# Attention feeding a gated FFN on one core: the last q slice in a lent PSUM bank, and k^T v joined to q times k^T v

## The chip, the cores and the metric

The kernel runs on one core of one Trainium2 chip. The core has five engines with queues of their own: TensorE (PE; PEld is its weight load), VectorE (DVE), ScalarE (ACT), GpSimd (POOL) and SyncE (SP), which only issues DMAs. On-chip memory is SBUF, 128 partitions; matmul results go to PSUM, whose banks hold 128 x 512 float32 each. The metric is the device time of one execution in microseconds, the lower the better.

## The reference

Eight batches of eight heads, 576 positions, head width 64. There is no softmax: k^T v is formed first, q is multiplied with it, each 64-wide row is normalised, and the result, heads side by side, is the input of a gated FFN (512 wide, 1536 inside, 4608 tokens in all).

```python
kv = np.einsum('bhsd,bhse->bhde', k, v)
out = np.einsum('bhsd,bhde->bhse', q, kv)
rms = np.sqrt(np.mean(out * out, axis=-1, keepdims=True) + 1e-06)
out = out / rms * g_norm
# (B,H,S,D) -> (B*S, H*D)
gate = 1.0 / (1.0 + np.exp(-(x @ w_gate)))
val = x @ w_val
return (gate * val @ w_out)
```

q, k and v come as 32-bit floats; the weights come as 64-bit floats, which the kernel converts itself.

## The kernel before

**The FFN.** The tokens are cut into nine chunks of 512 (`c` = 0 to 8). Chunk 0 goes through plain products (128x512 instructions, L599 and L833) while VectorE and ScalarE convert the weights, a step at a time (`CV`, the lines L197 to L237). Chunks 1 to 8 use a bilinear scheme with fewer multiplications: `first_layer_fast` runs three blocks `j` of 26 products each (list `PRODUCTS1`, four 128x256 instructions a product, L957), numbered p = 26 j + i from 0 to 77; `second_layer_fast` runs 26 longer products (L1059). Each product accumulates into a region, a PSUM bank named by a letter A to K; a region's bank is taken from the left of a deque `free` of five banks at its first product, and given back at the right after its last use. After each product, `combine` writes the steps listed with it: copies out of PSUM on ScalarE (L923; `o3=B` is one), sigmoids on ScalarE (L916), sums on VectorE (L927), multiplications on GpSimd (L919). GpSimd also forms the sums of h that the second layer multiplies (`h_sums`, L733), and in chunk 1 some of the sums of the output weights (`w_form`: L1030 on either engine, L1032 on VectorE alone).

**Attention.** Batch 0 is done at the start, head pair by head pair. Batches 1 to 7 are done inside the FFN of an earlier chunk: batches 1 and 2 begin in chunk 0, batch c + 1 runs in chunk c. `feed(b)` makes the steps. A batch is worked in two runs `m` = 0, 1 of four heads each:

- `load_q_run` loads q of one run into a tile: 32-column pieces of two head pairs, so that one 32x32-block transpose on VectorE turns them; behind these 2 S columns lie 2 HD more, a second copy of the last two rows of each group, of the head pair that otherwise lies on the upper 64 partitions (L119, L120). `load_late` loads k and v of the next batch into h_more, which later holds sums of h.
- `kv_mm` forms k^T v of all eight heads in one tile `at` of three PSUM banks: 64 instructions of 128x64 (the mains, L389), then 16 of 64x64 (the rest of the rows, L396). `kv_copy` brings it to SBUF on ScalarE, once whole (L404) and once more from the upper 64 partitions to the lower (L405). `kv_set_aside` (batch 2) copies it to a place of its own first (L400).
- `turn` transposes q (L408; the second copy L410).
- `u_mm` multiplies (L439): nine slices of 128 rows for each of two head pairs `g` and each half `e`, 64x64 matmuls. Head pair g sits on partitions 64 g to 64 g + 63, hence on that row half of the array; e sets the column half. Slices 0 to 7 of g = 0 land in one bank, those of g = 1 in the next; the last slices of both land side by side in the third, and the last slice of g = 1 is taken from the second copies of q and k^T v, on row half 0.
- `u_square` squares the whole of u (L444, ScalarE, PSUM to SBUF), `u_sum` sums over 64 (L447), `u_root` takes the root, and the normalisation and the transposes to the FFN's layout follow.

**What sets the order.** No scheduler moves anything; the code runs in the order in which the program writes it, engine by engine. Around the change three lists set it: `places` (chunk 0: "44:KV2,ASIDE" is the step list behind the 44th plain product instruction), `where` (from batch 2 on: "28:u0" puts u of run 0 behind product 28 of the first layer), and the list `forms` of chunk 1 (product, sum, engine). Each step that an engine is not ready for makes it wait, and what stands behind waits too.

Of the kernel before, what the change touches and what calls it, by code (L numbers as in the profile page):

```python
# [10 lines left out]
FP32 = mybir.dt.float32  # L11
# [9 lines left out]
def kernel(  # L21
# [32 lines left out]
    JR = S // QB  # L54
    NSL = JR // 2
    NRUN = NHP // 2
    QW = 2 * S + 2 * HD

    NK4 = S // P
    S4 = P * NK4  # L60
# [44 lines left out]
    def load_q_run(b, m):  # L105
        if b >= B:
            return
        if b == 1:
            t = h_main[2 - m].rearrange("p s c -> p (s c)")[:, 4 * NT * P - QW:4 * NT * P]
        else:  # L110
            t = sb.tile([P, QW], FP32, tag="q", name="q", bufs=1)
        main = t[:, 0:2 * S].rearrange("p (e j c) -> p e j c", e=2, c=QB)
        more = t[:, 2 * S:QW].rearrange("p (e j c) -> p e j c", e=2, c=QB)
# [152 lines left out]
    g_col = const.tile([P, 1], FP32, name="g_col")  # L266


    kvq = const.tile([P, 2, NRUN, 2, HD], FP32, name="kvq")
# [20 lines left out]
    def attention(n, at_ps):  # L290

        b, m = divmod(n, NHP)
        d = {}
        kv = kvq[:, 0, m // 2, m % 2]

        def kv_mm():
            d["kv"] = ps = at_ps("kv")
# [78 lines left out]
    def feed(b):  # L376

        d = {}

        def kv_mm():  # L380

            mains, rest = kv_late[b]
            d["kv"] = ps = at_ps()[:, 0:NRUN, 0:2 * HD].rearrange("p m (e d) -> p m e d", d=HD)
            for m in range(NRUN):
                for e in range(2):
                    for j in range(NK4):
                        for g in range(2):
                            c = slice(NK4 * HD * e + HD * j, NK4 * HD * e + HD * j + HD)
                            nc.tensor.matmul(ps[HD * g:HD * g + HD, m, e], mains[2 * m + g, "k"][:, c],  # L389
                                             mains[2 * m + g, "v"][:, c],  # L390
                                             start=(e == 0 and j == 0), stop=False, skip_group_check=True)
            for e in range(2):
                for m in range(NRUN):
                    for g in range(2):
                        rs, c = slice(PH * m, PH * m + PH), HD * (2 * g + e)
                        nc.tensor.matmul(ps[HD * g:HD * g + HD, m, e], rest[rs, c:c + HD],  # L396
                                         rest[rs, GH + c:GH + c + HD], start=False, stop=True, skip_group_check=True)

        def kv_set_aside():
            nc.scalar.copy(out=kv_ahead, in_=d["kv"])  # L400
            d["kv"] = kv_ahead

        def kv_copy():
            nc.scalar.copy(out=kvq[:, 0], in_=d["kv"])  # L404
            nc.scalar.copy(out=kvq[0:HD, 1], in_=d["kv"][HD:P])  # L405

        def turn(m, e):
            nc.vector.transpose(qTs[:, S * e:S * e + S], q_late[b, m][:, S * e:S * e + S])  # L408
            if e == 1:
                nc.vector.transpose(qTs[0:HD, 2 * S:QW], q_late[b, m][0:HD, 2 * S:QW])  # L410
                if b > 1:
                    load_q_run(b + (m + 1) // NRUN, (m + 1) % NRUN)
                elif m == NRUN - 1:
                    load_q_run(b + 1, 0)

        def heads_run(m):
# [6 lines left out]
            def place(g, s_):  # L423
                return (NSL - 1) * g + s_ if s_ < NSL - 1 else 2 * (NSL - 1) + g
# [2 lines left out]
            def by_head(t):  # L427
                return t.rearrange("p (n d) -> p n d", d=HD)

            def u_mm():  # L430
                d["u"] = u = at_ps().rearrange("p r c -> p (r c)")[:, 0:2 * S]
                for t in range(NSL + 1):
                    for g in range(2):
                        if t < NSL - 1 or g == 0:
                            head, s_ = (1, NSL - 1) if t == NSL else (g, t)
                            o = HD * place(head, s_)
                            for e in range(2):
                                c = 2 * S + HD * e if t == NSL else S * e + HD * s_
                                nc.tensor.matmul(u[HD * e:HD * e + HD, o:o + HD],  # L439
                                                 qTs[HD * g:HD * g + HD, c:c + HD],  # L440
                                                 kvq[HD * g:HD * g + HD, t == NSL, m, e], start=True, stop=True)

            def u_square():
                nc.scalar.activation(out=sq, in_=d["u"], func=AF.Square)  # L444

            def u_sum(i):
# [44 lines left out]
        kv = [kv_mm, kv_copy, kv_set_aside] if b == 2 else [kv_mm, kv_copy]  # L491
        t0, t1 = ([lambda m=m, e=e: turn(m, e) for e in range(2)] for m in range(NRUN))
        u0, u1 = heads_run(0), heads_run(1)
        if b == 1:
            return kv, t0 + t1 + u0 + u1, ()
        n_ = "n{0}0 n{0}1 n{0}2 n{0}3 n{0}4 n{0}5 n{0}6" if b == 2 else "n{0}0 n{0}1"
# [71 lines left out]
    def at_ps():  # L568
        return psum.tile([P, NAT, 512], FP32, tag="at", name="at")
# [212 lines left out]
    def w1_form(c, j, part, v):  # L782
        if c == 1:
# [13 lines left out]
    named = {"LL": lambda: load_late(1), "LL2": lambda: load_late(2), "KV": batch1[0][0], "KV2": second_batch[0][0],  # L797
             "W0": lambda: w1_sums(0), "W1": lambda: w1_sums(1),
             "ASIDE": second_batch[0][2], "CV": convert_step}
    named.update({"C": batch1[0][1], "D": second_batch[0][1]})  # L800
    for i in range(NRUN):
        named[f"Q{i}"] = lambda i=i: load_q_run(1, i)
        named.update({f"t{i}{e}": batch1[1][2 * i + e] for e in range(2)})
    for i, which in enumerate("ab"):
        for n, step in enumerate(("u", "sq", "s0", "s1", "rt", "rc", "n0", "n1", "n2", "x0", "x1")):
# [326 lines left out]
    for c in range(1, NG):  # L1132
        at1, at2 = {}, {}
        for p, step in x_late:
            at1.setdefault(p, []).append(step)
        x_late = []
        if c + 1 < B:
            kv, first_, then = second_batch if c == 1 else feed(c + 1)
            for p, step in (list(zip((21, 22) if c == 2 else (19, 20), kv)) if c > 1 else []) + first_:
                at1.setdefault(p, []).append(step)  # L1140
            for p, step in zip((3, 6) if c == 1 else (4, 6), then):
                at2.setdefault(p, []).append(step)
        if c + 1 < NG:
            for n, p in enumerate(X1 if c == 1 else X2 if c + 1 < B else X3):
                step = lambda n=n, c=c: x_sum(c + 1, n)
                if p < NPR:
                    at2.setdefault(p, []).append(step)
                else:
                    x_late.append((p - NPR, step))
        if c == 1:  # L1150
            for at_, forms in ((at1, ((28, 9, 0), (30, 10, 0), (34, 12, 0), (52, 11, 1), (53, 22, 0), (57, 14, 0), (58, 8, 1), (61, 19, 0), (64, 16, 1))), (at2, ((1, 13, 0), (3, 23, 0), (4, 25, 1), (9, 15, 0), (10, 24, 0), (10, 20, 0), (11, 17, 0), (12, 18, 0), (13, 21, 0)))):
# [36 lines left out]
```

## Time and profile before

| | |
|---|---|
| time, median of 3 runs | 1002.54 us (1002.2 to 1002.74) |
| the profiled execution's own time | 1003.68 us |
| its span | 1001.9 us, TensorE's granted clock 1.00 |
| PE busy | 993.2 us, 99% |
| VectorE, GpSimd, ScalarE busy | 723.3, 617.8, 342.2 us |
| chunk 0 from the first q times k^T v, 62.6 to 162 | 99.4 us |
| chunk 1, 162 to 262.57 | 100.57 us |
| chunks 2 and 3 | 106.63 and 106.64 us |

A line of a group reads: line of the kernel, engine, operation, tiles out <- in, shape, count, busy time, mean duration, idle time of the engine ahead of it and what ended it. A line of a tile's answer has the shortest, median and longest duration in ns instead. A line of the waits reads: who waited, for whom, the total in us, how often, and the longest one. A piece of the chain is: start, length, engine and line. A line of a timeline has start and length of a run of instructions of one line, and in square brackets how long its engine idled before it. Several matmuls overlap in the array, so counts and starts tell more of their pace than durations.

### The profile page before, as it was taken

What the parts mean: (1) busy time and instruction counts of PE and PEld (TensorE: products, weight loads), DVE (VectorE), ACT (ScalarE), POOL (GpSimd) and SP (SyncE); (2) the same over time, 40 slices, a digit from 0 to 9 for tenths busy, and PEclk for the clock granted to TensorE, in tenths of its full rate; (3) what the DMA queues carried; (4) which work ended last, traced back from release to release, by engine and by line L of the source; (5) the groups of instructions that cost most, each with busy time, mean ns of one, the idle gap of its engine ahead of it and who ended that gap; (6) DMA issues with size and microseconds to landing.
All of it is one profiled execution on the core that took longest, in us unless ns stands there. A gap on an engine that the chain in (4) does not pass through costs nothing.

```text
span 1001.9 us, 16623 instructions
## 1 busy us (share of the span) xinstructions
PE 993.2 (99%) x5958; PEld 815.9 (81%) x5958; DVE 723.3 (72%) x1199; ACT 342.2 (34%) x606; POOL 617.8 (62%) x991
## 2 busy tenths in 40 slices
PE   8999999999999999999999999999999999999998
PEld 7445447888888888888888888888888888888887
DVE  4889999889757756784677576866587566755672
ACT  4566322652144213530344124421442133213320
POOL 1509997798259633965196708861596349744963
PEclk9999999999999999999999999999999999999999
DMA  9996514764899568746975677756754555444614
GB/s 256 285 263 192 173 42 119 220 220 134 271 294 267 176 183 239 240 158 197 278 220 170 186 218 244 196 171 193 235 198 159 161 176 208 157 148 162 216 50 124
DMA packets 155155, 195.43 MB, mean 195 GB/s; under 512 B 83809, under 2 KB 127841, under 8 KB 155073
## 3 DMA queue, kind: packets, MB, share of 16 engines
q0 software_dynamic: 22128, 114.37, 34.4%
q1 hardware_dynamic: 126864, 78.16, 27.9%
q10 hardware_dynamic: 6080, 1.84, 0.8%
q8 instruction: 47, 0.77, 0.3%
q14 instruction: 36, 0.29, 0.1%
HBM read 160.50 MB, written 25.56 MB: 186 GB/s over the span
## 4 chain that ended last, share of the span: by engine, by line
PE 94%; POOL 2%; DMA 1%; ACT 1%; SPq 1%; issue 1%; DVE 1%; POOLq 0%; ACTq 0%; DVEq 0%
PE mm L957 51%; PE mm L1059 27%; PE mm L599 8%; PE mm L833 4%; PE at L439 2%; PE at L389 1%; DMA v<-in_v_dram 1%; PE at L599 1%; POOL h_more L733 1%; POOL h L733 1%; POOL h L919 0%; POOL w L1030 0%; SPq L93 0%; PE at L396 0%; DVE sg L927 0%
## 5 line engine op out<-in xcount | busy, mean ns | idle before, releaser
L957 PE MATMUL mm<-xs,w 128*128 128x256 f32 x1428 | 331.9, 380 | 0.0
L957 PEld LDWEIGHTS mm<-xs,w 128*128 128x128 f32 x1428 | 270.4, 190 | 37.4 <-DVE sg L927 0.4
L957 PE MATMUL mm<-xT,w 128*128 128x256 f32 x948 | 229.8, 380 | 0.0
L957 PEld LDWEIGHTS mm<-xT,w 128*128 128x128 f32 x948 | 179.5, 190 | 25.0 <-issue 0.2
L780 POOL DMA_DIRECT2D w<-kept x84 | 46.7, 556 | 192.5 <-PE mm L957 188.5
L927 DVE TENSOR_TENSOR sg<-sg,mm 128x512 f32<-128x512 f32 (+1 forms) x176 | 100.8, 600 | 85.0 <-PE mm L957 40.3
L1059 PE MATMUL mm<-w,h 128*128 128x256 f32 x630 | 142.8, 379 | 0.0
L1059 PEld LDWEIGHTS mm<-w,h 128*128 128x128 f32 x630 | 119.7, 190 | 16.3
L919 POOL TENSOR_TENSOR h<-h,sg 128x512 f32<-128x512 f32 x72 | 96.7, 1360 | 56.4 <-DVE h L927 30.4
L923 ACT COPY temps<-mm 128x512 f32<-128x512 f32 (+1 forms) x128 | 66.1, 538 | 186.7 <-PE mm L1059 94.7
L733 POOL TENSOR_TENSOR h<-h 128x128 f32<-128x128 f32 x216 | 113.1, 535 | 16.5 <-DVE h_more L733 13.1
L1059 PE MATMUL mm<-w,h_more 128*128 128x256 f32 x474 | 108.2, 379 | 0.0
L916 ACT ACTIVATE sg<-sg 128x512 f32<-128x512 f32 x96 | 59.7, 630 | 133.6 <-DVE sg L927 133.6
L1059 PEld LDWEIGHTS mm<-w,h_more 128*128 128x128 f32 x474 | 90.1, 190 | 12.2
L923 ACT COPY sg<-mm 128x512 f32<-128x512 f32 (+1 forms) x112 | 56.9, 510 | 86.4 <-PE mm L1059 45.0
L733 POOL TENSOR_TENSOR h_more<-h 128x128 f32<-128x128 f32 x120 | 61.6, 517 | 35.0 <-DVE h L919 30.8
L927 DVE TENSOR_TENSOR temps<-temps,mm 128x512 f32<-128x512 f32 (+1 forms) x96 | 59.4, 619 | 25.7 <-PE mm L1059 16.5
L599 PE MATMUL mm<-xT,w 128*128 128x512 f32 x176 | 77.8, 596 | 0.1
L927 DVE TENSOR_TENSOR temps<-mm,temps 128x512 f32<-128x512 f32 (+1 forms) x64 | 39.8, 622 | 50.7 <-PE mm L1059 24.3
L923 ACT COPY h<-mm 128x512 f32<-128x512 f32 x48 | 28.1, 585 | 138.3 <-PE mm L957 138.3
L927 DVE TENSOR_TENSOR sg<-mm,sg 128x512 f32<-128x512 f32 (+1 forms) x64 | 39.7, 620 | 46.7 <-PE mm L957 24.7
L599 PEld LDWEIGHTS mm<-xT,w 128*128 128x128 f32 x176 | 32.6, 190 | 39.2 <-issue 36.1
(148 smaller groups left out, 1283.6 us busy)
## 6 DMA issues: line engine op xcount, KB each, us to landing
w<-kept POOLq DMA_DIRECT2D x42, 896.0 KB, 5.4
w<-kept POOLq DMA_DIRECT2D x90, 384.0 KB, 4.8
w<-kept POOLq DMA_DIRECT2D x42, 768.0 KB, 5.0
out_dram<-sg SPq DMA_DIRECT2D x119, 64.0 KB, 1.7
h_more<-in_k_dram SPq DMA_DIRECT2D x28, 256.0 KB, 5.5
h_more<-in_v_dram SPq DMA_DIRECT2D x28, 256.0 KB, 6.2
q<-in_q_dram SPq DMA_DIRECT2D x96, 72.0 KB, 5.0
xT<-xTs SPq DMA_DIRECT2D x96, 72.0 KB, 4.6
```

What stands on the lines that cost most here:

```text
L389: nc.tensor.matmul(ps[HD * g:HD * g + HD, m, e], mains[2 * m + g, "k"][:, c], mains[2 * m + g, "v"][:, c], start=(e == 0 and j == 0), stop ...
L439: nc.tensor.matmul(u[HD * e:HD * e + HD, o:o + HD], qTs[HD * g:HD * g + HD, c:c + HD], kvq[HD * g:HD * g + HD, t == NSL, m, e], start=True ...
L599: nc.tensor.matmul(self.ps[i], w[("wg", "wv")[i], self.f][:, m, :], xT[self.c][:, m, :], start=(m == 0), stop=(m == NMT - 1), skip_group_c ...
L733: ops.append((eng, lambda v=v, x=x, sign=sign, y=y, eng=eng: eng.tensor_tensor(out=h_form(v, j), in0=h_form(x, j), in1=h_form(y, j), op=op ...
L780: nc.gpsimd.dma_start(out=granule(g)[:, 0:n], in_=kept1[g // NPA % N3, g % NPA][:, 0:n])
L833: nc.tensor.matmul(ps[t], gv[0, f][:, P * t:P * t + P], w["wo", f], start=(f == 0), stop=(f == NFT - 1), skip_group_check=True)
L916: nc.scalar.activation(out=o["o" + step[1]], in_=o["o" + step[1]], func=AF.Sigmoid)
L919: mult.tensor_tensor(out=o[x], in0=o[x], in1=o[y], op=ALU.mult)
L923: nc.scalar.copy(out=o[out_], in_=o[expr])
L927: tt(out=o[out_], in0=o[x], in1=o[y], op=ALU.add if sign == "+" else ALU.subtract)
L957: nc.tensor.matmul(regions[name][1][:, g], ws[:, g], xf[c][wv], start=(new and g == 0), stop=True, skip_group_check=True)
L1059: nc.tensor.matmul(regions[name][1], h_form(hv, j), ws[:, j], start=(used[i] and j == 0), stop=(j == N3 - 1), skip_group_check=True)
```

## The change

- q's second copies are no longer loaded or transposed (`QW` = 2 S), nor k^T v's. The last slice of g = 1 goes, like the others of g = 1, through row half 1, into the first 64 columns of another bank: bank 4 for batch 1, and from batch 2 on a bank lent from the deque `free` while u is formed. Just ahead of the square ScalarE copies these 128x64 values to their place beside the others, and the bank goes back to `free`.
- From batch 3 on `kv_mm` and `kv_copy` are no steps of their own; they run inside run 0's `u_mm`, which stands behind product 25 in place of 28 (k^T v stood behind 19, or 21 in chunk 2). The 64x64 part goes first, then the mains of m = 0 and m = 1; m = 0 is formed in the third bank of `at`, m = 1 in the lent bank, beside the slice that will come there. Two 128x128 copies to SBUF follow in place of a 128x256 and a 64x256 copy, and then u. The square stays behind product 30.
- In chunk 0 batch 2's k^T v (KV2) is formed inside `bu` (u of batch 1, run 1), which stands at place 44 in place of 47; the square of it goes to 47, with the setting aside behind it.
- In chunk 1 sum 14 of the output weights (VectorE) stands behind product 55 in place of 57, with its store.

```diff
-    QW = 2 * S + 2 * HD
+    QW = 2 * S
...
-                queue.dma_start(out=more[QB * i:QB * i + QB, e], in_=src[:, JR - 2:JR])
...
-        def kv_mm():
+        def kv_mm(at, lent):
...
+            if at is None:
+                at = at_ps()
+                d["kv"] = ps = [at[:, m, 0:2 * HD].rearrange("p (e d) -> p e d", d=HD) for m in range(NRUN)]
+            else:
+                d["kv"] = ps = [t.rearrange("p (e d) -> p e d", d=HD)
+                                for t in (at[:, NAT - 1, 2 * HD:4 * HD], lent[:, HD:3 * HD])]
...
+            if b > 2:
+                tails(True)
...
         def kv_copy():
-            nc.scalar.copy(out=kvq[:, 0], in_=d["kv"])
-            nc.scalar.copy(out=kvq[0:HD, 1], in_=d["kv"][HD:P])
+            for m in range(NRUN):
+                nc.scalar.copy(out=kvq[:, m], in_=d["kv"][m])
...
-                nc.vector.transpose(qTs[0:HD, 2 * S:QW], q_late[b, m][0:HD, 2 * S:QW])
...
+            def u_mm(first=()):
+                at = at_ps()
+                d["u"] = u = at.rearrange("p r c -> p (r c)")[:, 0:2 * S]
+                i_ = 4 if b == 1 else free.popleft()
+                lent = bank(i_)
+                for step in first:
+                    step(at, lent)
+                for s_ in range(NSL):
                     for g in range(2):
...
+                        o = HD * place(g, s_)
+                        to = lent[:, 0:HD] if s_ == NSL - 1 and g == 1 else u[:, o:o + HD]
...
+                d["lent"] = i_, lent[:, 0:HD], u[:, o:o + HD]
 
             def u_square():
+                i_, lent, to = d["lent"]
+                nc.scalar.copy(out=to, in_=lent)
+                if b > 1:
+                    give(i_)
                 nc.scalar.activation(out=sq, in_=d["u"], func=AF.Square)
...
+            u0[0] = lambda u_mm=u0[0]: u_mm((kv_mm, lambda at, lent: kv_copy()))
+            kv = []
...
-                   5:t00 8:t01 28:u0 29:t10 30:q0 33:s00,s01 36:r0 39:t11 41:n00 47:n01 51:x00,x01 54:u1
+                   5:t00 8:t01 25:u0 29:t10 30:q0 33:s00,s01 36:r0 39:t11 41:n00 47:n01 51:x00,x01 54:u1
...
-                   3:t00 7:t01 28:u0,t10 30:q0,s00,s01 37:r0 39:t11 47:n00,n01 53:x00,x01 54:u1
+                   3:t00 7:t01 25:u0 28:t10 30:q0,s00,s01 37:r0 39:t11 47:n00,n01 53:x00,x01 54:u1
...
-        43:ax1 44:KV2,ASIDE 46:CV,W0 47:bu 48:CV,CV,bsq 50:CV,bs0 52:CV,CV 54:bs1 55:CV,CV,brt,D 57:CV,CV 58:CV 60:CV,brc
+        43:ax1 44:bu 46:CV,W0 47:bsq,ASIDE 48:CV,CV 50:CV,bs0 52:CV,CV 54:bs1 55:CV,CV,brt,D 57:CV,CV 58:CV 60:CV,brc
...
-                    (52, 11, 1), (53, 22, 0), (57, 14, 0), (58, 8, 1), ...
+                    (52, 11, 1), (53, 22, 0), (55, 14, 0), (58, 8, 1), ...
```

More of the change, by code (lines that the diff above doesn't have):

```diff
@@ L266 @@
     g_col = const.tile([P, 1], FP32, name="g_col")
-    kvq = const.tile([P, 2, NRUN, 2, HD], FP32, name="kvq")
+    kvq = const.tile([P, NRUN, 2, HD], FP32, name="kvq")
     kv_ahead = const.tile([P, NRUN, 2, HD], FP32, name="kv_ahead")
@@ L293, in attention @@
         d = {}
-        kv = kvq[:, 0, m // 2, m % 2]
+        kv = kvq[:, m // 2, m % 2]
         def kv_mm():
@@ L378, in feed, with tails @@
         d = {}
-        def kv_mm():
+        def kv_mm(at, lent):
             mains, rest = kv_late[b]
-            d["kv"] = ps = at_ps()[:, 0:NRUN, 0:2 * HD].rearrange("p m (e d) -> p m e d", d=HD)
+            if at is None:
[4 more added lines that the diff above has]
+                                for t in (at[:, NAT - 1, 2 * HD:4 * HD], lent[:, HD:3 * HD])]
+            def tails(first):
+                for e in range(2):
+                    for m in range(NRUN):
+                        for g in range(2):
+                            rs, c = slice(PH * m, PH * m + PH), HD * (2 * g + e)
+                            nc.tensor.matmul(ps[m][HD * g:HD * g + HD, e], rest[rs, c:c + HD],
+                                             rest[rs, GH + c:GH + c + HD], start=first and e == 0, stop=not first,
+                                             skip_group_check=True)
+            if b > 2:
+                tails(True)
             for m in range(NRUN):
@@ L388, in kv_mm @@
                             c = slice(NK4 * HD * e + HD * j, NK4 * HD * e + HD * j + HD)
[L389 to L397, printed above, removed]
+                            nc.tensor.matmul(ps[m][HD * g:HD * g + HD, e], mains[2 * m + g, "k"][:, c],
+                                             mains[2 * m + g, "v"][:, c], start=(b < 3 and e == 0 and j == 0),
+                                             stop=(b > 2 and j == NK4 - 1), skip_group_check=True)
+            if b < 3:
+                tails(False)
         def kv_set_aside():
-            nc.scalar.copy(out=kv_ahead, in_=d["kv"])
-            d["kv"] = kv_ahead
+            for m in range(NRUN):
+                nc.scalar.copy(out=kv_ahead[:, m], in_=d["kv"][m])
+            d["kv"] = [kv_ahead[:, m] for m in range(NRUN)]
         def kv_copy():
-            nc.scalar.copy(out=kvq[:, 0], in_=d["kv"])
-            nc.scalar.copy(out=kvq[0:HD, 1], in_=d["kv"][HD:P])
+            for m in range(NRUN):
+                nc.scalar.copy(out=kvq[:, m], in_=d["kv"][m])
         def turn(m, e):
@@ L804 @@
     for i, which in enumerate("ab"):
-        for n, step in enumerate(("u", "sq", "s0", "s1", "rt", "rc", "n0", "n1", "n2", "x0", "x1")):
+        for n, step in list(enumerate(("u", "sq", "s0", "s1", "rt", "rc", "n0", "n1", "n2", "x0", "x1")))[which == "b":]:
             named[which + step] = batch1[1][2 * NRUN + 11 * i + n]
@@ L1138 @@
             kv, first_, then = second_batch if c == 1 else feed(c + 1)
-            for p, step in (list(zip((21, 22) if c == 2 else (19, 20), kv)) if c > 1 else []) + first_:
+            for p, step in first_:
                 at1.setdefault(p, []).append(step)
```

27 lines of the change are left out of this document (11 added, 16 removed).

## The prediction, made before the result was known

> **What bounds the kernel now.** I read the page's busy shares first, then TensorE's waits, then the chain of waits over one batch, then groups and timelines around the lines that change.
>
> ```profile
> PE 993.2 (99%) x5958; PEld 815.9 (81%) x5958; DVE 723.3 (72%) x1199; ACT 342.2 (34%) x606; POOL 617.8 (62%) x991
> ```
>
> ```profile
> PE mm L652 <- POOL ident masks.py:199: 1.4, 1, 1.4
> PE mm L301 <- DMA v<-in_v_dram: 1.3, 2, 0.8
> ...
> PE mm L957 <- POOL h L733: 0.4, 1, 0.4
> ```
>
> PE is busy 99% of the span, and its waits sum to about 4 us, nearly all before 30 us. After that one wait is left, of 0.4 us, in chunk 1. So from 30 us on only two things count: PE time added or removed, and new PE waits. The chain for chunk 3, start and length in us, is PE alone:
>
> ```profile
> 369.20 17.27 PE mm L957 x80
> 386.47 2.02 PE at L389 x64
> 388.49 0.39 PE at L396 x16
> 388.88 7.97 PE mm L957 x36
> 396.85 1.31 PE at L439 x72
> 398.16 22.64 PE mm L957 x104
> 420.80 1.31 PE at L439 x72
> 422.11 20.05 PE mm L957 x92
> 442.17 33.67 PE mm L1059 x156
> ```
>
> The last line gives 216 ns for one 128x256 instruction (33.67/156). The small matmuls are three trips out of the long stream: one to k^T v (L389, L396), two to q times k^T v (L439). From 369.20 to 442.17 are 72.97 us; 312 product instructions at 0.2158 are 67.33, the small pieces 2.41 + 2 x 1.31 = 5.03; the 0.61 left is the cost of going and returning, **0.20 us a trip**.
>
> ```profile
> L439 PE MATMUL at<-kvq,qTs x1008: 218/218/267, 61.2 to 742.0; 64*64 64x64 f32 x168
> L396 PE MATMUL at<-h_more x112: 218/218/267, 52.9 to 708.6; 64*64 64x64 f32 x112
> L444 ACT ACTIVATE sqs<-at x14: 1130/1131/1137, 62.7 to 742.9; 128x1152 f32<-128x1152 f32 x14
> L404 ACT COPY kvq<-at x6: 350/372/373, 53.7 to 708.8; 128x256 f32<-128x256 f32 x6
> L405 ACT COPY kvq<-at x6: 368/368/369, 54.0 to 709.2; 64x256 f32<-64x256 f32 x6
> ```
>
> One L439 trip is 72 instructions. In the trace's rows the first 64 start in groups of four, a group each 58 ns (16 groups); the last 8 start in pairs, a pair each 58 ns (4 pairs). The pairs are the last slices of the two head pairs, which both go through the array's first 64 rows now.
>
> **The change part by part.** The sum is made against the profiled execution (1003.68 us, span 1001.9, 1.8 around it); the median, 1002.54, is 1.14 below it.
>
> *Last slice through the lent bank.* The last 8 instructions become 2 groups of four, at 2 x 58 = 0.117 us less per trip; 14 trips (2 for each of 7 batches): **-1.64 us**. Bounds: 0 if the two halves don't run side by side into two banks; -1.64 if they do, as the first 16 groups do.
>
> *k^T v joined to u0, batches 3 to 7.* One trip of three goes: -0.20 each, **-1.0 us** for five. The pieces keep their lengths: 64x64 ahead of 128x64, then 64x64 again, has one change of shape more than 128x64 ahead of 64x64. A change costs 0.09 us in the rows (151 ns where 58 is the pitch), and the product after a trip starts 0.10 late; so four changes in place of five and one late product in place of two are again 0.19. In chunk 0 KV2 is joined into bu with its mains still ahead of its tails, so three changes are left of five: 2 x 0.09 for the changes, 0.10 for the late product and 0.05 for the late first group behind a change: **-0.33**.
>
> *What the joined u waits for.* u's first matmul waits for the first k^T v copy on ScalarE. That copy can start when the first run's mains are done, half way through L389's 2.02 us; behind it lie the other 1.0 us of mains, the copy takes under 0.37 (L404 has 256 columns, this 128), and ScalarE's sigmoid before it (393.29 to 393.92) ends with product 25. Cover 1.0 us, need about 0.4: 0. The second copy (128x128, nearest rows L404 372 and L479 342) starts as u starts and is needed only by the last slice, 0.93 us on: 0. Without that cover (u behind both copies) it would be about 0.55 us a batch. GpSimd's first write over k and v in h_more comes 5.9 us after product 25, the reads end at 3: 0.
>
> *Removed.* L405's copies, 7 x 0.37 us of ScalarE, replaced by the second 128x128 copy; 14 transposes at L410 (0.26 us) of VectorE; 56 DMA issues (four for each of 14 runs; 48 on SP's queue with the x stores and out stores behind them, 8 on GpSimd's for batch 1). ScalarE, VectorE and SP are not the bound: 0 here, but VectorE sits 0.26 us earlier behind each.
>
> *Added: 14 copies 128x64 on ScalarE, just ahead of the square.* Duration: 512 columns took 585 ns, 256 took 372, so 64 about 212 (estimate); the nearest row of this size, L479, took 292 to 461. They matter where ScalarE is late. With u at product 25 and the square still at 30, ScalarE runs: copy A, copy C, lent copy, square, copy B (o3=B); and product 32 writes bank B again. In the timeline of chunk 3 before:
>
> ```profile
> 396.88 0.58 ACT L923 COPY h<-mm 128x512 f32<-128x512 f32 x1 [1.14 <-PE mm L957]
> ...
> 398.20 1.13 ACT L444 ACTIVATE sqs<-at 128x1152 f32<-128x1152 f32 x1 [0.74 <-PE at L439]
> ...
> 399.23 0.58 ACT L923 COPY sg<-mm 128x512 f32<-128x512 f32 x1
> ```
>
> The first of these is copy C, the last copy B. Before, u's trip stood between C and product 29 and gave ScalarE 1.5 us. After, on the same clock: C 396.88, lent copy 0.48 later (the pitch of copies), square 0.21 later, B 1.03 later, done 0.58 later: 399.2. Product 32 follows C's product by three products and would have its weights by 399.1: a stall of 0.09 us (0 to 0.25, with the 461 row) each, five times, and once in chunk 1: **+0.54**.
>
> *Chunk 0.* PE saves 2 x 0.117 + 0.33 = 0.57, but the second half of chunk 0 is paced by VectorE's weight conversion (96.37 of 99.40 us busy from 62.6 to 162). The saving lasts only as far as conversion leaves room, about 0.2 us at product 4 of the second layer; and the ASIDE copies and the square now stand ahead of ScalarE's part of one conversion. I keep 0.2 (bounds -0.57 to +0.3 against before): **+0.37** back.
>
> *w_out sum 14, two products sooner in chunk 1.* VectorE, before:
>
> ```profile
> 210.09 1.41 DVE L447 TENSOR_REDUCE ms<-sqs 128x9 f32<-128x576 f32 x2 [1.28 <-ACT sqs L444]
> 211.42 1.95 DVE L1032 SCALAR_TENSOR_TENSOR w<-w,w 128x768 f32<-128x768 f32 x1
> ```
>
> PE's only late wait (a gap of 0.79 where 0.22 is the pitch, so 0.57) is at 226.94 behind a GpSimd sum of h, and that chain starts from VectorE, which runs about 2.6 us late there. After, sum 14 stands ahead of the reduces, in the 1.28 us that VectorE waited. Its other rows took 0.95 and 1.20. If it runs in the gap, VectorE is up to 1.86 us earlier behind it; if it is held until GpSimd's multiplication ends at 209.95, it ends at 210.9 and VectorE is 1.0 earlier. By the first the wait goes wholly; by the second the wait goes too, but narrowly, since PE itself comes 0.34 earlier. The next limit on GpSimd's own chain lies 0.72 below the present one. I take -0.6 for chunks 0 and 1 together, of which 0.2 and 2 x 0.117 - 0.09 are counted above: **-0.26** more.
>
> The Trainium skill, "SBUF — State Buffer", section "Who interferes with whom", has a VectorE instruction with two SBUF inputs blocked by a GpSimd instruction that reads SBUF. This trace bears it out (GpSimd's L1030 sums, 1.8 us elsewhere, took 2.26 beside such work). By it VectorE is 1.0 us earlier, without it 1.86.
>
> **Sum.** -1.64 - 1.0 - 0.33 + 0.54 + 0.37 - 0.26 = -2.3. 1003.68 - 2.3 = 1001.4 by the profile, **1000.2** by the median.
>
> **Rivals.**
> 1. *The wait at 226.94 stays* (another GpSimd sum is late). Then chunks 0 and 1 end where they did, and only the five batches count: 5 x (0.234 + 0.20 - 0.09) = 1.7: **1000.8**. For it: GpSimd works without a break from 216 to 228. Against: its chain hangs on VectorE.
> 2. *Everything pays*: no stall at product 32, and chunks 0 and 1 give all that GpSimd's next limit allows: 5 x 0.434 + 0.72 = 2.9: **999.6**. For it: the stall is 0.1 by the sum, and only if the weights wait and not the product. Against: VectorE in chunk 0 has no room.
> 3. *The halves don't overlap* in the lent bank: -1.64 goes, the lent copy remains: -0.7, **1001.9**. For it: no row shows a group of four into two different tiles. Against: the first groups of four write different banks too.
> 4. *Slower: ScalarE at product 32.* If lent copy and square go one after the other with a wait for PSUM between, or the lent bank comes back late and product 29 has no bank, each batch loses the excess: above 0.46 us per batch (2.3/5) it decides; at 0.8 (one square's remainder and a lost pitch of 0.5) five batches cost 5 x 0.8 - 2.3 = +1.7, and chunk 0's conversion another 0.5: **1004.7**. For it: slack was only 0.1 there. Against: ScalarE is 34% busy, and catches up within two products.
>
> **How the numbers follow.** Forecast 0.45, rival 1 0.20, rival 2 0.10, rival 3 0.08, rival 4 0.17. The forecast's own range is 999.7 to 1000.8 (the stall at 0 to 0.25 six times, rival 1's bound above). The range takes in rivals 1 to 3 and the better part of what lies between 3 and 4, and leaves out most of 4; below, it goes 0.5 past rival 2, for the trip cost being a mean: 999.1 to 1002.9. 0.2% of 1002.54 is 2.0 us, about what can be told from no change: 1000.5 and 1004.5. Faster: two thirds of the forecast, rival 2, and a third of rival 1, 0.47; slower: most of rival 4, 0.13; the rest 0.40.
>
> **What would show it.** L439 1.31 to 1.19 us per trip and 64x64 matmuls in groups of four to the end; one trip fewer in each of chunks 2 to 6, their length 106.63 to about 106.3; ScalarE's B copy ending at product 32's start, with a new PE wait on L923 of about 0.1; no PE wait behind L733 in chunk 1. Wrong if PE's waits list shows L439 behind L404's copies, or any wait over 0.4 us per chunk.

## The result, and the profile after

Measured side by side, 21 executions each, the kernel before took 1003.2 us (median) and the changed one 1000.77 (999.4 to 1003.04); the ratio is 0.9971, 95% interval 0.9964 to 0.9979, which is 2.1 to 3.6 us less on 1002.54. The forecast, 1000.2 from 1002.54, is a ratio of 0.9977. The changed kernel is faster, and inside the range. The measured ratio puts it at 999.6 on the forecast's scale, 2.9 us less; the forecast's 2.3 lies inside the interval too.

The profiled execution of the changed kernel took 1003.04 us, span 1001.3: the slowest of its 21, and only 0.64 us below the one shown of before. So spans of two profiles can't be compared here; the stretches within them can. The line numbers move by the lines that were added: L439 is now L453, L389 L403, L396 L392, L957 L980, L1059 L1082, L923 L946, L927 L950, L733 L755, L444 L462, L1032 L1055; the lent copy is L459. Some of the runs below shift them by a few lines more.

PE is busy 99% of the span, as before. Its waits, after:

```profile
PE two L353 <- DVE sqs L345: 1.5, 1, 1.5
PE mm L674 <- POOL ident masks.py:199: 1.4, 1, 1.4
PE mm L856 <- DVE w L235: 0.6, 2, 0.3
PE two L309 <- DMA q<-in_q_dram: 0.6, 1, 0.6
PE two L326 <- ACT qTs L314: 0.6, 2, 0.3
```

The wait behind GpSimd's h (L733 before) is gone from the list. L856, the plain second layer of chunk 0, waits twice for converted weights, at 117 and 124 us; that is new. The other four stand in the first 25 us, where the kernel before waited in much the same places. The chain over chunk 3, from the first product to the second layer:

```profile
369.76 22.45 PE mm L980 x104
392.21 0.20 PE at L392 x2
...
392.60 1.08 PE at L403 x32
393.68 0.93 PE mm L403 x32
394.62 1.14 PE at L453 x66
...
395.82 25.34 PE mm L980 x116
421.16 1.14 PE at L453 x66
...
422.37 20.05 PE mm L980 x92
```

Two trips where there were three. k^T v (L392, then L403, first into `at`, then into the lent bank, here named mm) runs straight into u (L453), and the last slice alternates between `at` and mm in pieces of two.

Between landmarks in the trace's rows (first product of one layer to the first of the next; chunk 0 from its first k^T v instruction at about 50 us) the two profiled executions compare like this, in us:

| stretch | before | after | difference |
|---|---|---|---|
| chunk 0, from the first k^T v | 106.842 | 108.147 | +1.305 |
| chunk 1, first layer | 71.004 | 70.258 | -0.746 |
| chunks 2 to 5, first layer, each | 72.962 | 72.664 | -0.298 |
| chunk 6, first layer | 73.218 | 72.664 | -0.554 |
| each second layer | 33.670 | 33.670 | 0 |

From the end of chunk 0 on the change is worth 0.746 + 4 x 0.298 + 0.554 = **2.49 us**. Chunk 0 is the odd one: in three other executions with the same chunk 0 (q0_at_31, tails_last, sum14_back below) it took 106.77 to 106.80, so -0.04 to -0.07. With those, the whole is -2.5 to -2.6, inside the measured 2.1 to 3.6. The 108.15 is one execution's own; with it the two profiled executions differ by 1.2 only.

### The profile page after: what moved, and what is told of

It reads as the page before. It is cut to its first block, busy times and chain, and to the rows that moved or that the text cites. A ratio compares the mean times of both kernels' runs of the same rounds, so it can differ in the third digit from the quotient of the medians.

```text
span 1001.3 us, 16581 instructions
## 1 busy us (share of the span) xinstructions
PE 992.3 (99%) x5958; PEld 815.3 (81%) x5958; DVE 721.1 (72%) x1185; ACT 342.8 (34%) x621; POOL 610.0 (61%) x983
## 4 chain that ended last, share of the span: by engine, by line
PE 93%; DVE 4%; issue 1%; DMA 1%; SPq 1%; ACT 0%; DVEq 0%; ACTq 0%
PE mm L980 54%; PE mm L1082 27%; PE mm L621 5%; PE mm L856 3%; PE at L453 2%; DVE cz L226 1%; DVE w L222 1%; PE at L403 1%; DMA st<-in_moe_w_val_dram 1%; DVE w L195 1%; PE mm L403 1%; DVE cz L210 0%; DVE w L235 0%; DVE h L629 0%; SPq L100 0%
## 5 line engine op out<-in xcount | busy, mean ns | idle before, releaser
L980 PE MATMUL mm<-xs,w 128*128 128x256 f32 x1428 | 331.8, 380 | 0.0
L980 PEld LDWEIGHTS mm<-xs,w 128*128 128x128 f32 x1428 | 270.5, 190 | 37.9 <-ACT sg L946 1.2
L980 PE MATMUL mm<-xT,w 128*128 128x256 f32 x948 | 230.6, 380 | 0.0
L980 PEld LDWEIGHTS mm<-xT,w 128*128 128x128 f32 x948 | 179.5, 190 | 25.0 <-issue 0.5
L950 DVE TENSOR_TENSOR sg<-sg,mm 128x512 f32<-128x512 f32 (+1 forms) x176 | 100.8, 600 | 75.6 <-PE mm L980 34.4
L1082 PE MATMUL mm<-w,h 128*128 128x256 f32 x630 | 142.8, 379 | 0.0
L1082 PEld LDWEIGHTS mm<-w,h 128*128 128x128 f32 x630 | 119.7, 190 | 16.3
L946 ACT COPY temps<-mm 128x512 f32<-128x512 f32 (+1 forms) x128 | 66.2, 540 | 184.7 <-PE mm L1082 94.7
L755 POOL TENSOR_TENSOR h<-h 128x128 f32<-128x128 f32 x216 | 111.4, 528 | 16.5 <-DVE h_more L755 13.1
L1082 PE MATMUL mm<-w,h_more 128*128 128x256 f32 x474 | 108.2, 379 | 0.0
L1082 PEld LDWEIGHTS mm<-w,h_more 128*128 128x128 f32 x474 | 90.1, 190 | 12.2
L946 ACT COPY sg<-mm 128x512 f32<-128x512 f32 (+1 forms) x112 | 56.5, 511 | 84.1 <-PE mm L1082 45.3
L755 POOL TENSOR_TENSOR h_more<-h 128x128 f32<-128x128 f32 x120 | 58.5, 491 | 34.0 <-DVE h L942 29.7
L950 DVE TENSOR_TENSOR temps<-temps,mm 128x512 f32<-128x512 f32 (+1 forms) x96 | 59.5, 620 | 26.1 <-PE mm L1082 16.8
L950 DVE TENSOR_TENSOR temps<-mm,temps 128x512 f32<-128x512 f32 (+1 forms) x64 | 39.9, 623 | 53.0 <-PE mm L1082 23.9
L946 ACT COPY h<-mm 128x512 f32<-128x512 f32 x48 | 28.1, 586 | 142.9 <-PE mm L980 129.4
L950 DVE TENSOR_TENSOR sg<-mm,sg 128x512 f32<-128x512 f32 (+1 forms) x64 | 39.7, 620 | 41.3 <-PE mm L1082 21.6
```

Source lines behind the costliest of these rows:

```text
L755: ops.append((eng, lambda v=v, x=x, sign=sign, y=y, eng=eng: eng.tensor_tensor(out=h_form(v, j), in0=h_form(x, j), in1=h_form(y, j), op=op ...
L946: nc.scalar.copy(out=o[out_], in_=o[expr])
L950: tt(out=o[out_], in0=o[x], in1=o[y], op=ALU.add if sign == "+" else ALU.subtract)
L980: nc.tensor.matmul(regions[name][1][:, g], ws[:, g], xf[c][wv], start=(new and g == 0), stop=True, skip_group_check=True)
L1082: nc.tensor.matmul(regions[name][1], h_form(hv, j), ws[:, j], start=(used[i] and j == 0), stop=(j == N3 - 1), skip_group_check=True)
```

## The experiments

The first question was which part of the change brings what; the second, what the 0.1 us at product 32 is and whether it can be had back; the third, what chunk 0 does. The times of these runs scatter by one to three us whatever the edit (more on that at the end), so the stretches above are the finer measure, and each conclusion rests on them. A gap is the time from the start of one product instruction to the start of the next; 0.216 us is the usual one, the pitch. The diffs show only what matters; of a long line they show the part that changes.

**The lent bank alone.** To the kernel before: `u_mm`, `u_square` and `load_q_run` as in the changed kernel, k^T v apart.

```diff
...
-                queue.dma_start(out=more[QB * i:QB * i + QB, e], in_=src[:, JR - 2:JR])
...
+                        to = lent[:, 0:HD] if s_ == NSL - 1 and g == 1 else u[:, o:o + HD]
...
+                nc.scalar.copy(out=to, in_=lent)
...
```

> The kernel before, with the lent bank alone: last slice through row half 1, copy ahead of the square, no second q and k^T v; k^T v as a step of its own where it stood, u0 at 28, sum 14 at 57, chunk 0 in its old order. Theory (the rounds pay, 0.104 us a trip as the trace of the changed kernel shows): L439's trips take 1.208 in place of 1.312, all 14, -1.46 us; no new gap at product 32 in chunks 2 to 6, as u's trip stands between copy C and product 29 again; chunks 2 to 5 take 106.42 in place of 106.63; ratio 0.9985. Rival (most of the gain is the joining, the lent copy's lateness eats the rounds): chunks 2 to 5 above 106.55, with new gaps, ratio 0.9995 or more.

Ratio 0.9987 (0.9977 to 0.9998), 1002.68 us. First layers of chunks 2 to 5 took 72.756 in place of 72.962: 0.103 a trip, with no gap at product 32. Chunk 0 fell by 0.207, two trips' worth. The wait in chunk 1 stayed, with a gap of 0.802. So the two row halves do run side by side into different banks, and the two saved rounds (groups of matmuls that start together) pay nearly what was said of them, 0.103 and not 0.117 a trip: the next product starts 0.148 us behind the last small matmul's start, before and after, and the last of a group of four starts 0.013 later than the last of a pair. In chunk 1 product 58 has a gap of 0.320 in its second instruction that it had not before, 0.104 more: ScalarE's copy that this product needs is late there, behind the lent copy (the gap grows with it in lent_twice, below). Not expected: chunk 6 took 72.755, though it had 0.26 more than its neighbours before (73.218).

**Sum 14 alone.** To the kernel before:

```diff
-            ... (57, 14, 0), ...
+            ... (55, 14, 0), ...
```

> The kernel before, with sum 14 of the output weights at product 55 in place of 57 and nothing else. Theory (VectorE's lateness is what GpSimd's chain and then PE wait for in chunk 1): the one long gap in chunk 1's first layer, 0.79 us between two product instructions where 0.22 is the pitch, closes to 0.22 or nearly; the first layer of chunk 1 takes 70.4 us in place of 71.0; chunks 2 to 6 stay at 106.63; time -0.57 us, ratio 0.9994. Rival (the gap closed in the changed kernel because the transposes, the copies or the DMAs of the second q went, not by the sum): the gap stays above 0.6 and the time is that of before.

Ratio 0.9984 (0.9975 to 0.9993). Chunk 1's first layer took 70.358 in place of 71.004, 0.646 less, with no gap left at its end; chunks 2 to 5 stayed at 72.962, chunk 6 at 73.273. VectorE around the sum, in this run:

```profile
207.24 2.02 DVE L1032 SCALAR_TENSOR_TENSOR w<-w,w 128x768 f32<-128x768 f32 x1
209.19 1.40 DVE L447 TENSOR_REDUCE ms<-sqs 128x9 f32<-128x576 f32 x2
210.51 0.67 DVE L927 TENSOR_TENSOR sg<-sg,mm 128x512 f32<-128x512 f32 x1
```

VectorE's idle 1.28 us ahead of the reduces is filled; the sum itself is no shorter (2.02 us, 1.95 before). L927 comes 54.28 us after the chunk's start, against 55.55 before (213.28): 1.27 earlier.

**Sum 14 back.** To the changed kernel, the same edit the other way.

> The changed kernel with sum 14 of the output weights back at product 57. Theory (its place alone opened and closed the wait in chunk 1): the gap of 0.5 to 0.9 at the last products of chunk 1's first layer is there again, that first layer takes 70.8 to 71.2 in place of 70.26. Rival (the removed 64x128 transposes and the joined k^T v give VectorE enough): it stays near 70.26.

A single execution took 1000.72 us. First layer of chunk 1 70.904, 0.646 more than the changed kernel's, and the old gap of 0.786:

```profile
225.56 1.10 PE L980 MATMUL mm<-xs,w_ring 128*128 128x256 f32 x4 [0.41 <-POOL h L755]
```

The place of this one sum opens and closes the wait, from either kernel.

**The 64x64 part of k^T v last.** To the changed kernel, for batches 3 to 7:

```diff
-            if b > 2:
-                tails(True)
...
-            if b < 3:
-                tails(False)
+            tails(False)
```

> The changed kernel, with the 64x64 part of k^T v behind the mains for batches 3 to 7 too (it was ahead). Theory (the mains of m = 1 are the cover under which the first k^T v copy runs): both copies can only start at the end of all k^T v, u's first matmul waits for the first and its last slice for the second; one change of shape fewer is worth 0.09 to 0.14, the wait costs 0.4 to 0.6 a batch: chunks 2 to 5 take 106.6 to 106.8 in place of 106.33, and PE's waits show L453 behind the copy; time +1.3 to +2.3 against the changed kernel, ratio 0.999. Rival (the copies are hidden anyway and changes of shape are what counts): chunks 2 to 5 take 106.2, ratio 0.9965.

Ratio 0.9994 (0.9982 to 1.0007). First layers of chunks 2 to 6 took 73.087, 0.42 more than the changed kernel's (with the second layer, 106.76). PE's waits of this run:

```profile
PE at L450 <- ACT kvq L413: 1.8, 5, 0.4
```

These are five waits of 0.4 us (L450 and L413 are L453 and L416, u and the copy of k^T v): u's first instruction stands behind the first copy. With the mains last, the second run's mains (0.93 us in the chain above) hide that copy whole, at the price of one change of shape. The cover was real, and without it the joining loses more (0.42) than it brought (0.20 a batch, below).

**The lent copy twice.** To the changed kernel:

```diff
-                nc.scalar.copy(out=to, in_=lent)
+                for _ in range(2):
+                    nc.scalar.copy(out=to, in_=lent)
```

> The changed kernel, with the lent copy written twice in a row. Theory (ScalarE's row of copy C, lent copy, square, copy B sets the gap at product 32): the gap grows from 0.320 by about one more copy's 0.1 to 0.2, to 0.42 to 0.52, in chunks 2 to 6 and at the place in chunk 1; five or six times 0.1 to 0.2, +0.5 to +1.2 us in all. Rival (fixed cost): the gap stays 0.320.

A single execution took 1001.37 us. In each of chunks 2 to 6 the gap at product 32 grew by 0.23: product 32's first instruction started 0.231 later than the pitch (0.447), and its second 0.104 later, as before. First layers 72.893, against 72.664. The two copies took 0.45 us together (a single one 0.22), so the gap grows by just what ScalarE's chain of copies and square grows. In chunk 1 product 58 grew by the same 0.23. It is the end of this chain, copy B, that PE meets at product 32.

**Copy and square one product later.** To the changed kernel:

```diff
-25:u0 28:t10 30:q0,s00,s01 37:r0
+25:u0 28:t10 31:q0,s00,s01 37:r0
...
-53:u1 56:q1 57:s10,s11
+53:u1 57:q1,s10,s11
```

> The changed kernel, with copy and square of u0 behind product 31 in place of 30 (batches 3 to 7; the sums behind them), and those of batch 2's u1 behind 57 in place of 56: so copy B goes ahead of them on ScalarE. Theory (copy B late behind lent copy and square is the 0.10 us gap ahead of product 32): the gap of 0.320 at product 32 becomes 0.216 in chunks 2 to 6 and in chunk 1; chunks 2 to 5 take 106.23 in place of 106.33; time -0.6 against the changed kernel, ratio 0.9965. Rival (the gap is a fixed cost of another kind, as that of the first product after a trip): it stays 0.320. Other rival: the square now stands later, the sums and the normalisation on VectorE follow later, and a new gap of 0.1 or more appears at one of products 33 to 60.

Ratio 1.0004 (0.9991 to 1.0016): the whole gain of the change is gone. First layers of chunks 2 to 6 took 73.154, 0.49 more, that of chunk 1 71.259, 1.0 more (gaps of 0.876 at product 60 and of 0.513 at product 76). PE waits elsewhere:

```profile
PE mm L980 <- ACT temps L946: 2.1, 6, 0.5
```

Product 32 is free of its gap, and product 34 has one of 0.709. ScalarE in chunk 3 shows why:

```profile
398.42 0.59 ACT L946 COPY sg<-mm 128x512 f32<-128x512 f32 x1 [0.65 <-PE mm L980]
398.90 0.22 ACT L459 COPY at<-mm 128x64 f32<-128x64 f32 x1
399.15 1.13 ACT L462 ACTIVATE sqs<-at 128x1152 f32<-128x1152 f32 x1
400.18 1.07 ACT L946 COPY temps<-mm 128x512 f32<-128x512 f32 x2
```

Copy B (398.42) goes ahead now, but the square has moved ahead of the two copies to temps, one of which (t8=C) product 34 needs. The second rival was right in effect, though it looked for the new gap behind VectorE's sums and not behind ScalarE.

**Copy and square four products sooner.** If ScalarE has no room after product 30, it has some before: between the second k^T v copy and copy A it idled 1.99 us (396.92 in the changed kernel's timeline, shown below). To the changed kernel, with chunk 0 in its old order (c0_apart, below):

```diff
-25:u0 28:t10 30:q0,s00,s01 37:r0
+25:u0 26:q0 28:t10 30:s00,s01 37:r0
...
-53:u1 56:q1 57:s10,s11
+53:u1 54:q1 57:s10,s11
```

> The changed kernel with chunk 0 in its old order (as c0_apart) and the lent copy and square right behind u in place of behind product 30: q0 at 26 for batches 3 to 7, q1 of batch 2 at 54; the sums stay where they are. Theory (ScalarE has room between u and copy A, none between copies B and t8=C, where q0_at_31 put them): the gap at product 32 becomes 0.216 and no other comes in its place; first layers of chunks 2 to 5 72.56 in place of 72.665, of chunk 1 70.15 in place of 70.26; -0.6 us against c0_apart, ratio 0.9950. Rival (the 0.104 at product 32 does not come from ScalarE): 72.665 stays. Other rival (the square now makes copy A late, which product 30 waits for): a gap at product 30 in place of the one at 32.

Ratio 0.9960 (0.9946 to 0.9974). First layers of chunks 2 to 6 took 72.558, 0.106 less, and the gap at product 32 is gone. In chunk 1 the second rival came true: 70.728 in place of 70.257, with a wait of 0.45 at product 56.

```profile
208.23 1.13 ACT L462 ACTIVATE sqs<-at 128x1152 f32<-128x1152 f32 x1 [0.23 <-DVE xTs L482]
209.26 1.07 ACT L946 COPY h<-mm 128x512 f32<-128x512 f32 x2
```

u1 stands at 53 there, two products nearer to copy A's use than u0 at 25, and the square first waits for VectorE's transposes to have read its buffer. So one more version, with that square at 55, behind copy A:

> As square_at_26, with the square of batch 2's u1 at 55 in place of 54, behind copy A. Theory (at each place ScalarE must finish the copy that a product waits for; at 55 copy A goes ahead of the square and copy C comes 0.8 us before product 57): no gap at 56 and none at 58 in chunk 1, its first layer 70.15; first layers of chunks 2 to 5 72.56; 0.6 us below c0_apart and 0.6 below square_at_26 from batch 2's part on; ratio 0.9950. Rival (GpSimd's own chain in chunk 1 gives back what ScalarE gains): 70.25, with a gap at the last products of that first layer.

Chunk 1 took 70.152 and chunks 2 to 6 72.558, as expected, with no gap left in any of them but those behind trips. From the first k^T v to the last product this version takes 943.40 us, against 944.04 of c0_apart below and 946.74 of before. Its time doesn't show it: 1000.77 us, ratio 0.9975 (0.9963 to 0.9986); its profiled execution reached the first k^T v only at 51.77 us, where c0_apart's did at 49.46. That it is the fastest in time is therefore not shown.

**Chunk 0 in its old order.** To the changed kernel:

```diff
-44:bu 46:CV,W0 47:bsq,ASIDE 48:CV,CV 50:CV,bs0
+44:KV2,ASIDE 46:CV,W0 47:bu 48:CV,CV,bsq 50:CV,bs0
```

> The changed kernel, with chunk 0 in its old order: batch 2's k^T v at 44 with its setting aside, bu at 47, square at 48. Theory (the order of ScalarE in chunk 0, with the copy, the square and two settings aside ahead of a gate, makes VectorE's conversions later by about 1.2 us, and they pace the second half of chunk 0): VectorE's wait for the gate near 82 us goes, the plain second layer has no gap or gaps that sum to under 0.5, though PE loses 0.33 of the joining; time 0.3 to 0.8 below the changed kernel, ratio 0.9965. Rival (the gaps at 117, 124 and 132 us in the changed kernel's profile came of that execution's late start alone): time 0.3 above the changed kernel, ratio 0.9975, and the same gaps where the start is as late.

Ratio 0.9955 (0.9942 to 0.9967), 999.74 us; the interval overlaps that of the changed kernel. Chunk 0 took 106.635, 0.207 below before (its two trips' rounds), with no gap in the second layer. In the joined order it took 106.77 to 106.80 in three executions, 108.15 in a fourth, and 106.28 in lent_twice, where the lent copy of chunk 0 is doubled too.

**The square behind the gate.** With k^T v still joined, this run was to tell which step of the joined order makes VectorE late:

```diff
-47:bsq,ASIDE 48:CV,CV 50:CV,bs0
+48:CV,CV,bsq,ASIDE 50:CV,bs0
```

> The changed kernel, with chunk 0's square of bu and the setting aside written behind the gate and the two conversion steps of place 48 in place of 47; k^T v stays joined. Theory (it is the gate's place behind them that counts): VectorE goes through the gate's product near 82 us without the 1.4 us more, conversion ends 0.7 to 1.3 us sooner against the start of chunk 0, the second layer's gaps go or sum to under 0.5, and PE keeps the 0.33 of the joining: ratio 0.9960 to 0.9965. Rival (start alone, or the setting aside itself is late and holds something else): as the changed kernel, 0.9971.

Ratio 0.9959 (0.9945 to 0.9973), but chunk 0 took 106.761, as in the joined order: the theory fails. The last conversion ended 96.64 us after the first k^T v, where c0_apart had 95.33, the kernel before 96.42, and the joined order 96.63 to 96.68 (98.05 in the changed kernel's own profile, 95.55 in lent_twice). VectorE in c0_square_later, and below it in c0_apart:

```profile
81.70 0.69 DVE L629 TENSOR_TENSOR h<-mm,sg 128x512 f32<-128x512 f32 x1 [1.78 <-PE mm L621]
```

```profile
79.43 0.69 DVE L629 TENSOR_TENSOR h<-mm,sg 128x512 f32<-128x512 f32 x1
```

VectorE waits for PE, not for ScalarE: L629, its multiplication by the gate, takes the block whose last three products, 45 to 47, stand behind u since u stands at 44. Counted from the first k^T v, L629 starts at 31.02 us in place of 29.97.

That is one cause of the late conversion, but not the whole of it. In the one execution of lent_twice this multiplication (L630 there) starts at the same 31.02, and yet the chunk has no gap in its second layer and keeps the whole 0.36 of the joining (106.279 against 106.635). Two instructions behind L629 only about 0.3 of the 1.05 us is left, since the conversion between took 1.71 us in c0_apart and 1.33 in c0_square_later. From there on the lateness grows or shrinks with conversion rows that take one of two durations. Here is one of them, in lent_twice and below it in sum14_back:

```profile
102.39 1.21 DVE L226 SCALAR_TENSOR_TENSOR cz<-st,cz 128x1024 uint32<-128x1024 uint32 x1
```

```profile
101.99 1.74 DVE L226 SCALAR_TENSOR_TENSOR cz<-st,cz 128x1024 uint32<-128x1024 uint32 x1
```

Four rows later the same happens to L195: 0.65 in lent_twice, 1.14 in sum14_back. GpSimd's three sums beside these rows took 5.90 us in lent_twice and 5.11 in sum14_back, so what one engine has less the other has more; no run here moves GpSimd's sums to show that they decide it. So PE's 0.33 from the joining is lost in every execution of the joined order but that one, by a multiplication 1 us later together with conversion rows that then came out long.

**Both moves, later.** The edits of q0_at_31 and c0_square_later together:

> The changed kernel with the edits of c0_square_later and q0_at_31 together. Theory (they are independent): gaps at product 32 gone and chunk 0's conversion as early as in the kernel before; ratio 0.9955 to 0.9960, which would be the fastest version. Rival (either gives its gain back in chunk 1, where GpSimd's sums pace PE): a gap at the last products of chunk 1's first layer takes up what chunk 0 gains; ratio 0.9965 or more.

Ratio 1.0008 (0.9997 to 1.0019), with the stretches of its two halves: chunk 0 106.854, chunk 1 71.245, chunks 2 to 6 73.155. So the theory fails with both its halves; the two edits add up, and neither changes what the other does.

## Why the prediction was right, point by point

- *PE is the bound, only PE time and new PE waits count*: held. The 14 transposes and 56 DMA issues that went, and the copies that got shorter, left no trace of their own in chunks 2 to 5: the rounds measured alone (0.206), the forecast's 0.20 for the joining and one late product (0.104) make 0.302, and 0.298 was measured. One reading was wrong: after 30 us there was not one PE wait left but two, the second in chunk 6 (last point).
- *Rounds, -1.64*: right in kind, 0.103 a trip measured for 0.117, so -1.45. The rival that the halves don't overlap is out.
- *Joining, -0.20 a batch*: 0.298 - 0.206 + 0.104 = 0.196, as forecast.
- *u waits for no copy*: held. No L453 stands in PE's waits, and tails_last shows what the cover hides, 0.4 us. The other sign of being wrong, a wait over 0.4 us in a chunk, did come up in the changed kernel's own profile, in chunk 0 (L856, 0.6 in two waits); three other executions had gaps there that sum to 0.5.
- *Product 32, +0.09 each*: 0.104 to 0.106 by the gap and by what square_at_26 had back. ScalarE's chain came out as added up:

```profile
396.92 0.59 ACT L946 COPY h<-mm 128x512 f32<-128x512 f32 x1 [1.99 <-PE mm L980]
398.65 0.59 ACT L946 COPY h<-mm 128x512 f32<-128x512 f32 x1 [1.14 <-PE mm L980]
399.13 0.22 ACT L459 COPY at<-mm 128x64 f32<-128x64 f32 x1
399.38 1.13 ACT L462 ACTIVATE sqs<-at 128x1152 f32<-128x1152 f32 x1
400.41 1.07 ACT L946 COPY sg<-mm 128x512 f32<-128x512 f32 x2
```

  Copy C at 398.65, lent copy 0.48 later, square 0.25 later (0.21 forecast), copy B 1.03 later, done at 401.0 (400.41 + 0.58); product 32 starts at 401.04 by the trace's rows. The sign that was named for it was wrong: no wait on L946 appears in the list; the 0.1 is seen only in the starts. That ScalarE "catches up within two products" holds where the square stands, and not one product later.
- *Sum 14, -0.26*: right in kind and shown from both sides, but the term was too small. The wait went whole and alone brought 0.646: chunk 1 gained 0.746 = 0.206 for two trips, 0.646 for the wait, less 0.104 for one late copy B. The forecast held chunks 0 and 1 to 0.6 together, under a next limit on GpSimd's chain at 0.72; c0_apart gained 0.95 there (0.207 and 0.747), so that limit did not bind. The lower of the two values for VectorE, 1.0 us earlier, was the better one (1.27): the sum was held in its new place too, 2.02 us where another L1055 sum took 1.16 in the changed kernel. GpSimd's sum that began beside its end took 1.17 us (L755 at 211.41), and 0.46 before (L733 at 209.90). The Trainium skill, "SBUF — State Buffer", section "Who interferes with whom", says that a VectorE instruction with two SBUF inputs contends with a GpSimd instruction that reads SBUF. These rows agree with it, but no run here moves GpSimd's work to show it.
- *Chunk 0, 0.2 kept of 0.57*: too much by 0.13 to 0.16 against the three executions (0.04 to 0.07 kept), inside the bounds; the changed kernel's own profile, 1.3 longer than before, lies outside them. The reason was wrong. ScalarE's settings aside and the square cost nothing that moving them gives back (106.761); the step that failed is "the ASIDE copies and the square now stand ahead of ScalarE's part of one conversion". In its place stands what the forecast overlooked: three products of a block now lie behind u, and VectorE's multiplication of that block waits for them and starts 1.05 us later. That this alone costs the joining's gain is not shown: in lent_twice it starts as late, and the gain is kept. Why the one execution lost 1.3 us is only partly seen. PE itself fell 0.37 us behind inside u's trip, near 78.5 us, so that L629 waited 2.14 and not 1.78, and the conversion L222 at 88.39 took 1.78 us where c0_square_later's took 1.21. What held PE up there, and what set the conversion rows differently, is open.
- *Not foreseen: chunk 6, another -0.256.* Before, PE waited there once, at 738.96, and the page's list doesn't have it; the timeline does:

```profile
738.96 0.73 PEld L957 LDWEIGHTS mm<-xs,w 128*128 128x128 f32 x4 [0.39 <-DVE sg L927]
```

  It stayed with sum 14 alone (73.273) and went with the lent bank alone (72.755). So it goes with what the lent bank takes away or shifts. The 64x128 transposes that went are not the likely cause: VectorE's lateness in this chunk begins ahead of them, at a sum. Here it is before, and below it with the lent bank alone:

```profile
726.78 1.88 DVE L927 TENSOR_TENSOR h<-h,temps 128x512 f32<-128x512 f32 x1
```

```profile
724.30 1.07 DVE L943 TENSOR_TENSOR h<-h,temps 128x512 f32<-128x512 f32 x1
```

  Both start 37.8 us into the chunk. In chunks 3 to 5 before, the same sum took 0.93 to 1.23 us, with the transposes in place and no wait. GpSimd's sums of h run beside it; why it took 1.88 in chunk 6 is open.

The sum then, with the terms as measured: -1.45 (rounds), -0.98 (joining, batches 3 to 7), +0.63 (product 32, six times), -0.65 (sum 14), -0.26 (chunk 6); chunk 0's joining and the lateness that it costs VectorE give +0.14 to +0.17 beyond the rounds. That is -2.5 to -2.6. It lies close to the forecast's -2.3 in part by luck: sum 14 and chunk 6 brought 0.65 more than was said, the rounds, chunk 0 and product 32 about 0.4 less. Rival 2 (999.6) has the number of the measured ratio, but one of its two conditions failed: the stall at product 32 that it leaves out was there in each of the five batches.

## What to carry to other kernels

When one engine is busy 99% of the span, read the change as a list of what it does to that engine's rounds, trips and shapes, and as a list of the copies that its next instructions wait for; in chunks 2 to 5 both could be added up from a few rows to within a tenth of a microsecond a batch (0.34 said, 0.30 measured). A helper engine that is idle two thirds of the time can still have no room: moving 1.3 us of ScalarE's work by one product lost 0.5 us a batch, by four products the other way won 0.1. And where work is joined on the bound engine, ask what was to be finished just before it: three products left behind a trip made another engine's work start 1 us later, and all executions but one then lost what the joining had saved.

## What the runs showed that was not expected

- A product that meets the copy it waits for at about its own start pays 0.104 us: its first instruction starts on the pitch, its second 0.104 late (0.320 for 0.216), just as behind a trip. A copy 0.23 later adds 0.23 to that. (At products 60 and 76 of chunk 1, which waited longer, the second instruction was 0.075 late.) What makes the second instruction late is open.
- Most of the spread of the times lies ahead of the work that was changed. The first k^T v of a late batch started at 49.1 to 51.8 us in the thirteen profiled executions, with no order by kernel, while the first layers of chunks 2 to 5 repeat within 0.002 us. Take both the start and the stretch from there to the last product off an execution's time, and 6.05 to 6.46 us are left in all thirteen. A stretch of the trace told 0.1 us apart where the time of whole executions could not tell 1.
